# Half-size products of the second layer accumulated in PSUM, with copies on ScalarE and one wide addition; another order in the first layer's first step

## The chip, the cores and the metric

The kernel runs on one core of a Trainium2 chip. The metric is the device time of one execution in microseconds (us); less is better. An execution's time is a little more than the span from the first to the last instruction that the profile shows.

## The reference

```python
def _attn_ref(q, k, v, proj):             # 4 batches, 8 heads, 768 tokens, head size 64
    scale = 1.0 / np.sqrt(D)
    q_bits, k_bits = (einsum(x, proj) > 0 for x in (q, k))      # 6 bits each
    mask = q_bucket[:, :, :, None] == k_bucket[:, :, None, :]
    scores = np.where(mask, scale * q @ k.T, -1e9)
    attn = softmax(scores)
    return attn @ v

def _moe_ref(x, w_in, w_out):             # x: 3072 x 512, w_in: 512 x 2048, w_out: 2048 x 512
    h = x @ w_in
    g = h * (1.0 / (1.0 + np.exp(-1.702 * h)))
    return g @ w_out
```

The attention's output, transposed to (batch, token, head and feature), is the x of the feed-forward part. All of it is float32.

## The kernel before

**Three stages.** Attention fills the first 316 us. The first layer (`hidden`) runs to 606 us, in 24 steps: three blocks of 1024 tokens (`sb`) by eight blocks of 128 columns of each half of w_in (`mt`). The second layer (`product_of_halves`) takes the rest, in 21 steps: for each of the three token blocks the seven products `o` in the order `OUTER = (1, 2, 6, 7, 5, 3, 4)`. Numbered from 0, steps 0, 7 and 14 have o = 1, steps 5, 12 and 19 have o = 3, and steps 6, 13 and 20 have o = 4.

**Seven products instead of eight.** Both layers multiply matrices of 2 by 2 blocks with seven products, a scheme of the Strassen kind. Four sums of the left blocks and four of the right blocks are made first (`sums_a`, `sums_b`); the seven products are then combined by additions into the four output blocks c11, c12, c21, c22. The second layer does this twice, one scheme within the other: `OUTER` numbers the outer products, and each of them is made of seven inner products of half the size, `product(1)` to `product(7)`. `LEFT` and `RIGHT` say which block or sum each of these takes. Of the right operand, g: product 1 takes b11, 2 takes b21, 3 takes b22, 4 takes the sum t4, 5 takes t1, 6 takes t2, and 7 takes the second sum, which `sums_b` writes over b12. Of the left operand product 6 takes the sum s2 and product 3 the sum s4.

**One output step** (`product_of_halves(n, acc, after)`). Each inner product is eight TensorE instructions of 128 x 256 in the trace, into a bank of its own. ScalarE copies two of them out of PSUM (u and c12); VectorE combines the rest in half-size additions (128 x 256), and adds the quarters of an earlier product `acc` where the outer scheme wants that: o = 2, 6, 7, 3 and 4 have an acc, o = 1 and 5 have none. The result is `m`, four quarters of 128 x 256 in one of six buffers `wholes`.

**What stands between the products.** The callback `after(at)` places other VectorE work: `after(0)` runs what is pending from the step before (transposes of a finished block, `turned`, L831, and after o = 5 two wide additions, L991 and L992, the first of which is taken out ahead of the step with o = 3); `after(1)`, `after(2)` and `after(3)` make the sums of the next step's g, `g_sums(n + 1)`: t1 (L219), the second sum (L220), and then t2 (L221) and t4 (L222). In step 0 one sum goes to each of the four places. Finished blocks are written out by DMA (`written`, L838), and `fetch(n + 1)` (L806) loads the next g from DRAM into one of two buffers.

**Order of the work.** TensorE, VectorE, ScalarE and GpSimd (POOL) run their instructions in the order in which the program writes them (`tc.manual_schedule`); DMA issues on SyncE (SP) are ordered by the framework. GpSimd makes the sums of the left blocks (`inner_sums`, L211 to L214 for s1, s3, s2, s4). Before the GpSimd work of output steps 5 and 6 stands a one-element copy, so that this work waits for the product of the step before:

```python
                if n in (5, 6):
                    nc.gpsimd.tensor_copy(mark, ms[OUTER[n - 1]][0:1, 0, 0:1])
                for f in {0: inner_sums(4), 5: inner_sums(5) + inner_sums(6)[:2], 6: inner_sums(6)[2:]}.get(n, []):
```

Step 6 thus makes s2 and s4 of its own left operand.

**One hidden step.** `head(n)` makes product 1 and its copy u ahead of time, in the step before, so that product 6 can be accumulated onto the same bank; then 7 and 4 are accumulated there too, each after a copy by ScalarE (v, c22; c21 goes through the activation). Hidden step 0 has no step before it: its head stands directly ahead of product 6.

Of the kernel before, what the change touches and what calls it, by code (L numbers as in the profile page):

```python
# [38 lines left out]
def kernel(  # L39
# [17 lines left out]
    nc = tc.nc  # L57
# [8 lines left out]
    KC, FC = DM // P, FF // P  # L66
# [86 lines left out]
    for x in (0x3FFFFFFF, 0xFF800000):  # L153
        m = const.tile([P, 1], U32, name=f"mask_{x:x}")
# [61 lines left out]
    def sums_b(eng, b11, b12, b21, b22, t1, t2, t4):  # L216


        return [lambda: eng.tensor_tensor(t1, b12, b11, op=Alu.subtract),  # L219
                lambda: eng.tensor_tensor(b12, b22, b12, op=Alu.subtract),  # L220
                lambda: eng.tensor_tensor(t2, b22, t1, op=Alu.subtract),  # L221
                lambda: eng.tensor_tensor(t4, b21, t2, op=Alu.subtract)]  # L222
# [4 lines left out]
    def quarters_in(cols):  # L227
        w = [w_in_sb[:, K2 * k : K2 * (k + 1), F2 * i + cols.start : F2 * i + cols.stop]
             for i in range(2) for k in range(2)]
        return w + [s_in[:, i, :, cols] for i in range(3)]  # L230

    def quarters_x(sb):
        x = [xT[:, K2 * k : K2 * (k + 1), (2 * sb + j) * XT : (2 * sb + j + 1) * XT] for k in range(2) for j in range(2)]
        return x + [t_x[:, i] for i in range(3)]
# [460 lines left out]
    def feed_forward(tag, late=()):  # L695
# [3 lines left out]
        F4, TH = FC // 4, XT // 2  # L699
        n1 = N // (2 * XT)  # L700

        LEFT = dict(zip(range(1, 8), (0, 1, 6, 3, 4, 5, 2)))
        RIGHT = dict(zip(range(1, 8), (0, 2, 3, 6, 4, 5, 1)))
        OUTER = (1, 2, 6, 7, 5, 3, 4)
        with ExitStack() as fctx:
# [6 lines left out]
            def bank():  # L712
                turn[0] += 1
                return sets[turn[0] % 8 // 6 if len(sets) > 1 else 0].tile([P, XT], F32, tag="p", name="product")

            def product(ps, sb, mt, i, start=True):
                wq, xq = quarters_in(slice(mt * P, (mt + 1) * P)), quarters_x(sb)
                for kc in range(K2):
                    nc.tensor.matmul(ps, wq[LEFT[i]][:, kc, :], xq[RIGHT[i]][:, kc, :],  # L719
                                     start=(start and kc == 0), stop=(kc == K2 - 1), skip_group_check=not start)  # L720

            def head(n):

                ps, u = bank(), stage.tile([P, XT], F32, tag="u", name="u")
                product(ps, *divmod(n, FC // 2), 1)
                nc.scalar.copy(u, ps)  # L726
                return ps, u

            heads = {}

            def hidden(sb, mt, mid=(), end=()):
                n = sb * (FC // 2) + mt
                a, u = heads.pop(n) if n in heads else head(n)
                v, c12, c21, c22 = (stage.tile([P, XT], F32, tag=x, name=x) for x in ("v", "c12", "c21", "c22"))
                t2, t4 = (stage.tile([P, XT], F32, tag=x, name=x, bufs=1) for x in ("t2", "t4"))

                def keep(at, x):
                    loader[0].dma_start(out=g_dram[len(LEFT) * sb + at, :, mt, :], in_=x)

                def emit(c, at=None, of=None):  # L740
                    nc.scalar.activation(c, c if of is None else of, Act.Gelu_apprx_sigmoid)  # L741
                    if at is not None:
                        keep(at, c)

                product(a, sb, mt, 6, False)
                nc.scalar.copy(v, a)
                b = bank()
                product(b, sb, mt, 5)
                product(a, sb, mt, 7, False)
                nc.scalar.copy(c22, a)  # L750
                nc.vector.tensor_tensor(c22, b, c22, op=Alu.add)
                emit(c22, 3)
                c = bank()
                product(c, sb, mt, 2)
                nc.vector.tensor_tensor(u, c, u, op=Alu.add)
                emit(u, 0)
                if n + 1 < n1 * (FC // 2):
                    heads[n + 1] = head(n + 1)
                for x in mid:
                    x()  # L760
                product(a, sb, mt, 4, False)
                emit(c21, 2, a)
                product(b, sb, mt, 3, False)
                nc.vector.tensor_tensor(c12, b, v, op=Alu.add)  # L764
                emit(c12)

                for f, kept in zip(sums_b(nc.gpsimd, u, c12, c21, c22, v, t2, t4), ((4, v), (1, c12), (5, t2), (6, t4))):
                    f()
                    keep(*kept)
                for x in end:  # L770
                    x()
# [11 lines left out]
            def w_quarters(o):  # L783

                w = wqs[LEFT[o]]
                x = [w[:, i, F4 * j : F4 * (j + 1), :] for i in range(2) for j in range(2)]
                at = OUTER.index(o)
                if at == 0:
                    return x[0:2] + rooms[3:4] + x[3:] + rooms[0:3]
                return x + rooms[3 * at + 1 : 3 * at + 4]  # L790
# [8 lines left out]
            steps_out = [(sb, o) for sb in range(n1) for o in OUTER]  # L799
# [40 lines left out]
            def product_of_halves(n, acc, after):  # L840

                sb, o = steps_out[n]
                wq, gq = w_quarters(o), g_quarters(n)
                m = wholes[n % len(wholes)]
                u, v = (gp.tile([P, TH], F32, tag=x, name=x, bufs=2) for x in ("u", "v"))
                c11, c12, c21, c22 = (m[:, i] for i in range(4))

                def product(i):
                    ps = bank()[:, 0:TH]
                    for c in range(F4):  # L850
                        nc.tensor.matmul(ps, wq[LEFT[i]][:, c, :], gq[RIGHT[i]][:, c, :], start=(c == 0), stop=(c == F4 - 1))  # L851
                    return ps

                def add(dst, x, y):
                    nc.vector.tensor_tensor(dst, x, y, op=Alu.add)  # L855

                def corner():
                    add(c11, product(2), u)
                    if acc is not None:
                        add(c11, c11, acc[:, 0])  # L860


                final = n + 1 == len(steps_out)
                nc.scalar.copy(u, product(1))  # L864
                if not final:
                    corner()
                nc.scalar.copy(c12, product(3))
                after(0)
                add(v, product(6), u)
                add(c21, product(7), v)  # L870
                if acc is not None:
                    add(v, v, acc[:, 1])
                    add(c22, c21, acc[:, 3])
                    add(c21, c21, acc[:, 2])
                add(c12, c12, v)
                after(1)
                p = product(5)
                add(c22, p, c21 if acc is None else c22)
                add(c12, p, c12)
                after(2)  # L880
                if final:
                    corner()
                    after(4)
                add(c21, product(4), c21)
                after(3)
                return m
# [14 lines left out]
            for sb in range(n1):  # L901
                for mt in range(MT):
                    n = sb * MT + mt
# [45 lines left out]
            for n, (sb, o) in enumerate(steps_out):  # L949
                final = n + 1 == len(steps_out)  # L950
# [8 lines left out]
                m = wholes[n % len(wholes)]  # L959

                def after(at):
                    if at == 0:
                        while pending:
                            pending.pop(0)()

                    steps = [later_sums[at : at + 1]] if n == 0 else [[], later_sums[0:1], later_sums[1:2], later_sums[2:], []][at : at + 1]

                    if n + 2 >= len(steps_out):
                        turns = [lambda q=q: turned(m, int(final), int(not final), q, q + 1) for q in range(4)]
                        if final:  # L970
                            steps = [[[], [], [turns[1], turns[3]], [turns[2]], [turns[0]]][at]]
                        elif at == 3:
                            steps = [later_sums[2:3], turns[0:2], turns[3:4], later_sums[3:], turns[2:3]]
                    for f in sum(steps, []):
                        f()
                    if final and at in (2, 3):
                        written(sb, 0, (3 - at,), loader + [nc.scalar])
                    if n + 2 == len(steps_out) and at == 3:
                        written(sb, 1, (0, 1), loader + [nc.scalar])

                acc = {6: 1, 7: 6, 2: 1, 3: 6, 4: 7}.get(o)
# [70 lines left out]
```

## Time and profile before

| | |
|---|---|
| median of 3 runs | 873.26 us (872.33 to 873.48) |
| the profiled execution | 872.87 us |
| its span | 871.0 us |
| granted TensorE clock, mean | 0.997 |
| TensorE busy, its matmuls of the first layer (L719), of the second (L851) | 857.9 us, 33% and 26% of the chain |
| VectorE, ScalarE, GpSimd busy | 661.4, 340.2, 311.6 us |
| output steps 1, 2, 6, 8 | 12.08, 14.04, 12.45, 12.08 us |

The span is the time from the first to the last instruction; what an execution takes beyond it lies outside the program's instructions. A busy TensorE is not TensorE at its peak. In output steps 1 to 20 the step's time is counted from the first matmul of its product 1 to that of the next step's.

### The profile page before, as it was taken

To read this page: it belongs to the slowest core of one execution; us is meant where nothing else is said; L and a number is where in the kernel's file an instruction comes from. 1 tells how busy PE (TensorE), PEld (TensorE's weight loads), DVE (VectorE), ACT (ScalarE), POOL (GpSimd) and SP (SyncE) were. 2 spreads that over 40 slices of the span, in tenths; PEclk is the share of its full clock that TensorE was granted. 3 is DMA by queue.
4 is the path that set the end of the run, shared out by engine and by line. 5 is a ranking of instruction groups with operands and counts; after the bars stand their busy time and mean duration, and the time that the engine had idled before them with its cause. 6 is when DMAs were issued, how large, how long until landed. Compare 5 with 4: busy or idle time off the path is not lost.

```text
span 871.0 us, 13350 instructions
## 1 busy us (share of the span) xinstructions
PE 857.9 (99%) x4845; PEld 499.2 (57%) x4845; DVE 661.4 (76%) x924; ACT 340.2 (39%) x567; POOL 311.6 (36%) x275
## 2 busy tenths in 40 slices
PE   9999999999999999999999999999999999999996
PEld 5444444444444444444444444445878888888885
DVE  4589999999999875457555556676788977897786
ACT  5866667776666643434334333433000000000000
POOL 4242234333223465665443344559903100000000
PEclk9999999999999999999999999999999999999998
DMA  5636645456652104665456655576744675467524
GB/s 127 96 57 109 104 84 85 84 99 117 99 97 61 56 2 157 205 208 181 172 198 197 217 181 172 190 254 223 271 156 158 199 243 201 163 209 243 194 97 99
DMA packets 169161, 132.09 MB, mean 152 GB/s; under 512 B 123616, under 2 KB 138112, under 8 KB 163712
## 3 DMA queue, kind: packets, MB, share of 16 engines
q1 hardware_dynamic: 166528, 129.70, 52.5%
q10 hardware_dynamic: 2560, 1.46, 0.8%
q8 instruction: 40, 0.66, 0.3%
q14 instruction: 33, 0.27, 0.1%
HBM read 79.69 MB, written 50.33 MB: 149 GB/s over the span
## 4 chain that ended last, share of the span: by engine, by line
PE 95%; DVE 3%; issue 0%; DMA 0%; ACT 0%; ACTq 0%; DVEq 0%
PE product L719 33%; PE product L851 26%; PE ps L432 18%; PE av L465 15%; DVE xT L855 1%; PE dn L486 1%; PE hash L408 1%; PE tp L366 1%; DVE y L831 1%; DMA k<-in_k_dram 0%; DVE v L855 0%; PE hash L373 0%; DVE t2a L221 0%; DVE raw_g L220 0%; ACTq L838 0%
## 5 line engine op out<-in xcount | busy, mean ns | idle before, releaser
L433 ACT ACTIVATE e<-ps 128x768 f32<-128x768 f32 x192 | 151.2, 812 | 25.7 <-PE ps L432 23.2
L432 PE MATMUL ps<-qT,kT 64*128 64x384 f32 x768 | 155.1, 482 | 0.0
L465 PE MATMUL av<-e,v 128*32 128x385 f32 x1536 | 128.0, 487 | 0.0
L719 PE MATMUL product<-xT,w_in_sb 128*128 128x512 f32 x288 | 127.8, 592 | 0.0
L440 POOL TENSOR_TENSOR acc<-e 128x768 f32<-128x768 f32 x32 | 51.7, 1617 | 194.4 <-ACT e L433 175.0
L719 PEld LDWEIGHTS product<-xT,w_in_sb 128*128 128x128 f32 x288 | 54.6, 190 | 69.0 <-issue 68.5
L465 PEld LDWEIGHTS av<-e,v 128*32 128x32 f32 x1536 | 48.6, 109 | 76.2 <-issue 74.9
L432 PEld LDWEIGHTS ps<-qT,kT 64*128 64x128 f32 x768 | 68.0, 187 | 38.5 <-issue 38.4
L719 PE MATMUL product<-t_x,s_in 128*128 128x512 f32 x192 | 86.4, 592 | 0.8 <-ACT u L726 0.8
L764 DVE TENSOR_TENSOR c<-product,v 128x512 f32<-128x512 f32 x24 | 16.6, 690 | 90.8 <-PE product L719 90.8
L219 POOL TENSOR_TENSOR v<-c,u 128x512 f32<-128x512 f32 x24 | 32.3, 1345 | 128.1 <-ACT c L741 128.1
L864 ACT COPY u<-product 128x256 f32<-128x256 f32 x21 | 7.8, 372 | 174.1 <-PE product L851 140.9
L719 PEld LDWEIGHTS product<-t_x,s_in 128*128 128x128 f32 x192 | 36.4, 190 | 47.1 <-issue 45.2
L432 PE MATMUL ps<-qf,kf 64*128 64x384 bf16 x384 | 62.9, 324 | 0.1
L741 ACT ACTIVATE c<-c 128x512 f32<-128x512 f32 x48 | 30.3, 630 | 72.3 <-DVE c L764 43.7
L441 POOL TENSOR_TENSOR acc<-acc,e 128x768 f32<-128x768 f32 x32 | 55.8, 1745 | 2.5
L446 DVE SCALAR_TENSOR_TENSOR acc<-e 128x768 f32<-128x768 f32 x32 | 47.7, 1489 | 5.1 <-ACT e L433 5.1
L719 PE MATMUL product<-t_x,w_in_sb 128*128 128x512 f32 x96 | 45.1, 592 | 0.0
L719 PE MATMUL product<-xT,s_in 128*128 128x512 f32 x96 | 45.1, 592 | 0.0
L750 ACT COPY c<-product 128x512 f32<-128x512 f32 x24 | 14.1, 586 | 66.3 <-PE product L719 66.3
L432 PEld LDWEIGHTS <-kf 64*128 64x128 bf16 x384 | 18.9, 94 | 35.1 <-issue 6.2
L448 DVE TENSOR_TENSOR acc<-acc,e 128x768 f32<-128x768 f32 x32 | 34.3, 1071 | 3.3
(206 smaller groups left out, 1513.4 us busy)
## 6 DMA issues: line engine op xcount, KB each, us to landing
raw_g<-g_dram SPq DMA_DIRECT2D x22, 1024.0 KB
s_in<-g_dram SPq DMA_DIRECT2D x20, 1024.0 KB
g_dram<-c SPq DMA_DIRECT2D x72, 256.0 KB
g_dram<-t SPq DMA_DIRECT2D x48, 256.0 KB
raw<-in_moe_w_in_dram SPq DMA_DIRECT2D x16, 512.0 KB
raw<-in_moe_w_out_dram SPq DMA_DIRECT2D x16, 512.0 KB
v<-in_v_dram SPq DMA_DIRECT2D x32, 192.0 KB
g_dram<-u SPq DMA_DIRECT2D x24, 256.0 KB
```

The costliest lines, as they stand in the source:

```text
L219: return [lambda: eng.tensor_tensor(t1, b12, b11, op=Alu.subtract), lambda: eng.tensor_tensor(b12, b22, b12, op=Alu.subtract), lambda: eng ...
L432: nc.tensor.matmul(ps[:, j, 0:HS], a[hs, keys], m[hs, cols], start=not last, stop=last)
L433: nc.scalar.activation(es[c][:, kt, :, 0:HS], ps[:, :, 0:HS], Act.Exp, scale=1.0 / D**0.5)
L440: nc.gpsimd.tensor_tensor(acc, es[c][:, 0, :, 0:HS], es[c][:, 1, :, 0:HS], op=Alu.add)
L441: nc.gpsimd.tensor_tensor(acc, acc, es[c][:, 2, :, 0:HS], op=Alu.add)
L446: nc.vector.scalar_tensor_tensor(acc, e[0], T * TINY, e[1], op0=Alu.add, op1=Alu.add)
L448: nc.vector.tensor_tensor(acc, acc, x, op=Alu.add)
L465: nc.tensor.matmul(av[D * j + d : D * j + d + 32, :], vt[:, t, j, d : d + 32], es[c][:, t, j, :], start=(t == 0), stop=(t == T - 1))
L719: nc.tensor.matmul(ps, wq[LEFT[i]][:, kc, :], xq[RIGHT[i]][:, kc, :], start=(start and kc == 0), stop=(kc == K2 - 1), skip_group_check=not ...
L741: nc.scalar.activation(c, c if of is None else of, Act.Gelu_apprx_sigmoid)
L764: nc.vector.tensor_tensor(c12, b, v, op=Alu.add)
L851: nc.tensor.matmul(ps, wq[LEFT[i]][:, c, :], gq[RIGHT[i]][:, c, :], start=(c == 0), stop=(c == F4 - 1))
```

## The change

In an output step (all but the last) products 1, 6, 7 and 4 are accumulated in one bank, one onto the other. ScalarE copies the bank's content out after each of them: u, v, c22, c21. Products 2, 3 and 5 have banks of their own and are added to the copies by VectorE. The order of the products becomes 1, 2, 6, 3, 7, 5, 4 (before: 1, 2, 3, 6, 7, 5, 4). Where there is an acc, its four quarters are added to `m` in one VectorE instruction of 128 x 1024 behind product 4, instead of in four of 128 x 256 in the course of the step. The places of `after(0)` to `after(3)` follow the products as shown. The last step keeps its order: 1, 3, 6, 7, 5, 2, 4.

In hidden step 0 product 5 is made ahead of product 6, and the head of step 1 stands between products 6 and 7 instead of behind product 2.

```diff
+                b = bank()
+                if n == 0:
+                    product(b, sb, mt, 5)
                 product(a, sb, mt, 6, False)
                 nc.scalar.copy(v, a)
-                b = bank()
-                product(b, sb, mt, 5)
+                if n == 0:
+                    heads[1] = head(1)
+                else:
+                    product(b, sb, mt, 5)
                 product(a, sb, mt, 7, False)
                 nc.scalar.copy(c22, a)
                 nc.vector.tensor_tensor(c22, b, c22, op=Alu.add)
...
-                if n + 1 < n1 * (FC // 2):
+                if n and n + 1 < n1 * (FC // 2):
                     heads[n + 1] = head(n + 1)
...
-                def product(i):
-                    ps = bank()[:, 0:TH]
+                def product(i, onto=None):
+                    ps = bank()[:, 0:TH] if onto is None else onto
                     for c in range(F4):
-                        nc.tensor.matmul(ps, wq[LEFT[i]][:, c, :], gq[RIGHT[i]][:, c, :], start=(c == 0), stop=(c == F4 - 1))
+                        nc.tensor.matmul(ps, wq[LEFT[i]][:, c, :], gq[RIGHT[i]][:, c, :], start=(onto is None and c == 0),
+                                         stop=(c == F4 - 1), skip_group_check=onto is not None)
                     return ps
...
+                if n + 1 < len(steps_out):
+                    a = product(1)
+                    nc.scalar.copy(u, a)
                     add(c11, product(2), u)
+                    product(6, a)
+                    nc.scalar.copy(v, a)
+                    add(c12, product(3), v)
+                    after(0)
+                    product(7, a)
+                    nc.scalar.copy(c22, a)
+                    after(1)
+                    p = product(5)
+                    add(c22, p, c22)
+                    add(c12, p, c12)
+                    after(2)
+                    product(4, a)
+                    nc.scalar.copy(c21, a)
                     if acc is not None:
-                        add(c11, c11, acc[:, 0])
+                        add(m, m, acc)
+                    after(3)
+                    return m
...
```

What is left of the old body is the last step's; it loses only the branches that it never takes.

More of the change, by code (lines that the diff above doesn't have):

```diff
@@ L855, in add @@
                     nc.vector.tensor_tensor(dst, x, y, op=Alu.add)
-                def corner():
+                if n + 1 < len(steps_out):
+                    a = product(1)
+                    nc.scalar.copy(u, a)
                     add(c11, product(2), u)
+                    product(6, a)
[11 more added lines that the diff above has]
+                    nc.scalar.copy(c21, a)
                     if acc is not None:
-                        add(c11, c11, acc[:, 0])
-                final = n + 1 == len(steps_out)
+                        add(m, m, acc)
+                    after(3)
+                    return m
                 nc.scalar.copy(u, product(1))
-                if not final:
-                    corner()
                 nc.scalar.copy(c12, product(3))
@@ L870, in product_of_halves @@
                 add(c21, product(7), v)
[L871 to L874, printed above, removed]
+                add(v, v, acc[:, 1])
+                add(c22, c21, acc[:, 3])
+                add(c21, c21, acc[:, 2])
                 add(c12, c12, v)
@@ L877, in product_of_halves @@
                 p = product(5)
-                add(c22, p, c21 if acc is None else c22)
+                add(c22, p, c22)
                 add(c12, p, c12)
                 after(2)
-                if final:
-                    corner()
-                    after(4)
+                add(c11, product(2), u)
+                add(c11, c11, acc[:, 0])
+                after(4)
                 add(c21, product(4), c21)
```

## The prediction

> **What bounds the kernel now.** I read the page first: engine shares, then the chain of work that ended last.
>
> ```profile
> PE 857.9 (99%) x4845; PEld 499.2 (57%) x4845; DVE 661.4 (76%) x924; ACT 340.2 (39%) x567; POOL 311.6 (36%) x275
> ...
> PE 95%; DVE 3%; issue 0%; DMA 0%; ACT 0%; ACTq 0%; DVEq 0%
> ```
>
> TensorE is the bound; the change leaves its matmuls as they are. So only TensorE's pauses and the tail can move the time. The waits of PE give two that touch the changed lines:
>
> ```profile
> PE product L851 <- DVE t2a L221: 1.7, 1, 1.7
> PE product L719 <- ACT u L726: 0.8, 1, 0.8
> ```
>
> Next, busy time by stretch, one stretch for an output step (first column after the stretch is its length):
>
> ```profile
> 618.23:630.31 12.08, 12.08 (x57) 10.64 (x56) 9.95 (x13) 0.74 (x2) 11.85 (x8) 1.00 0.85 308
> 630.31:644.35 14.04, 12.33 (x58) 10.56 (x57) 13.80 (x22) 0.74 (x2) 2.15 (x2) 1.00 0.51 186
> ...
> 680.61:693.06 12.45, 12.32 (x58) 10.56 (x56) 12.18 (x23) 0.74 (x2) 0.00 (x0) 1.00 0.46 150
> ```
>
> A step without a pause is 12.08 us, seven products of 1.725. Counting from 0, step 2 is 1.95 longer, step 6 0.37. Last, the timeline where steps meet, in light step 8 and around step 5:
>
> ```profile
> 705.50 0.41 DVE L855 TENSOR_TENSOR xT<-product,xT 128x256 f32<-128x256 f32 x1
> 705.84 1.21 DVE L221 TENSOR_TENSOR t2a<-raw_g,t1a 128x1024 f32<-128x1024 f32 x1
> ...
> 710.33 1.89 PE L851 MATMUL product<-t2a,w_in_sb 128*128 128x256 f32 x8
> ...
> 675.84 1.22 DVE L992 TENSOR_TENSOR t_x<-t_x,xT 128x1024 f32<-128x1024 f32 x1
> 675.98 1.11 POOL L955 COPY mark<-t_x 1x1 f32<-1x1 f32 x1 [5.80 <-DVE t_x L855]
> 677.05 1.27 POOL L213 TENSOR_TENSOR s_in<-w_in_sb,w_out_sb 128x512 f32<-128x512 f32 x1
> ```
>
> Read the first three with S = 705.15, the step's start: product 6, the fourth, starts at S+5.18 and reads t2, which VectorE ended at S+1.90. That slack is what the new order spends. The last three show POOL's little mark copy stretched to 1.11 beside a wide VectorE addition (its other one took 0.17), and then the sum s2 that stands behind it.
>
> **What goes and comes.** VectorE loses, in a step with an earlier product to add (acc), eleven half additions of some 0.42 and gets four plus one wide one (L991, same shape: 1.22): 4.6 becomes 2.9. ScalarE goes from two copies of 0.37 to four, in a stage where it is busy 0.74 of 12.08. None of that is on TensorE's path, so it earns nothing by itself. The copies stand between products on one bank: copy v ends some 0.6 after product 6 and product 7 comes 1.73 after it, since product 3 lies between; without that cover each would cost TensorE about 0.6. Accumulating at full rate is seen already: L719's product 4 onto a used bank is at 328.04, the next at 329.76, 1.72 for four matmuls, like the rest.
>
> **Hidden step 0.** Product 1 starts at 316.59; product 6 waits for copy u until 319.38 (1.08 more than 1.715 per product), and product 7 comes 0.08 late. With product 5 ahead, copy u (over at 319.23) is done before product 6 at 320.0, and the moved head covers copy v. Product 5's inputs were there (POOL's s1 ended at 313.75). The moved head issues four matmuls and one copy, no DMA, and is queued ahead of nothing that TensorE lacked. **-1.15**; all later stages follow TensorE.
>
> **Light steps.** In the new order product 6 is third, at S'+3.45, its weight load 0.22 earlier at S'+3.23 (S' is the start of the next step). Ahead of t2 VectorE now has the wide addition, which waits for product 4 and ScalarE's copy: copy starts S'+0.20 (a copy at 710.53 behind a product whose successor started at 710.33), ends +0.57, wide addition +0.60, t2 one pitch of 1.13 later (850.75 to 851.88 in the chain), ends +2.95; the load follows 0.12 later (637.22 to 637.34 in step 2), +3.07. **0**, with 0.16 to spare, and the step 2 pause shows 0.11 more (load 2.06 late, product 7 late by 1.95). Queued behind the waiting addition are t2 and t4 alone; t4 is needed last.
>
> **Step 2** (ends the 1.95 pause). In step 1 VectorE's half additions and POOL's sums stretch each other (1.48 for one of 0.42). New: product 5 ends, c22 at 628.79, c12 629.13, the second sum (it overwrites b12) 629.47. That takes 2.2 beside POOL (t1 took 2.28 at 666.77), the wide addition partly so, 1.6; t2 ends at 634.4, load 634.5 against 633.54: 0.96 late, 0.86 after the 0.11. **-1.1**; free of POOL t2 ends at 632.9 (-1.95), fully beside it 635.4 (-0.1). I take the middle since POOL's sums ended at 632.54.
>
> **Heavy steps 5, 12, 19** (o = 3): the pending wide addition and four transposes now come after product 3, which is fourth. From S: c12 at 7.10, +0.34, addition to transposes 1.26 (843.10 to 844.36), transposes 1.86, t1 1.13, c22 and c12 0.34 each, second sum 1.13, wide 1.13, t2 1.21: it ends at S+15.84 = S'+3.76, load S'+3.88, 0.65 late, less 0.11: **+0.55** at step 13 (bounds 0.3 and 0.9). At step 20 VectorE is the chain to the end, and there t2 starts at S'+2.55 = 852.74 where the chain has
>
> ```profile
> 850.75 1.13 DVE raw_g L220
> ...
> 852.21 1.13 DVE t2a L221
> ```
>
> (timeline: 852.13): **+0.6** on everything behind it (0.3 to 1.0).
>
> **Step 6.** POOL's mark (L955) reads c11 of the product before. That was final early in step 5; now the wide addition writes it last, at S'+2.63 = 683.24. Behind the mark stand s2 and s4 of this very step, and product 6 needs s2. Mark 1.11 as in the row, beside t2: 684.4; s2 beside t4 2.13 (a POOL sum beside VectorE at 668.05): 686.5; load 686.65 instead of 683.84, 2.7 after the 0.11, against 0.37 before: **+2.3**. With mark at 0.17 and s2 at 1.27 it is +0.5; s4 arrives in time for product 3 either way. [...]
>
> **Sum.** -1.15 - 1.1 + 0.55 + 0.6 + 2.3 = +1.2. The profiled execution took 872.87 (span 871.0, 1.87 around it), so 874.1; the median of the runs, 873.26, is 0.39 above it: 874.5.
>
> **Rivals.**
> - *Slower: step 2's pause stays.* If the second sum and the wide addition both run fully beside POOL, that term is -0.1 and the sum +2.2: 875.5. For it: 8 POOL instructions fill 11.85 of step 1's 12.08. Against: VectorE's work there shrinks. 0.2.
> - *Slower: t2 late in the light steps too.* Eleven of them have the wide addition ahead; it decides once t2 ends beyond S'+3.22. Were it 0.2 beyond that, 2.2 in all: 876.7. Against: 0.27 of slack from rows. [...] 0.12.
> - *Slower: transfers.* The y writes leave some 3.5 us later (787.9 for 784.41); if the fetch of raw_g is queued behind, t1 of step 15 waits and t2 comes up to 1.2 late: 875.7. Against: the fetch is ready first, at the end of product 7. 0.08.
> - *Faster.* POOL lets the mark and s2 through (+0.5), step 2's pause goes wholly (-1.95), heavy terms at their lower ends (0.6): -2.0, 871.3. 0.12.
> - *The new first step doesn't remove its wait* (product 5 or 6 lacks an input): +1.15, 875.6. All its inputs were there by 316.3. 0.03.
>
> **How the numbers follow.** About 0.2%, 1.75 us, is what a measurement can tell from no change. The forecast, +1.2, lies within; it has 0.45. Sums between the cases spread over the edges: faster 0.13, same 0.46, slower 0.41. All low ends add to -2.0, all high ends (0.8 for 1.15 in hidden step 0, 1.2 for transfers) to +4.9; both at once are unlikely, so the range is 871.4 to 877.6. The likeliest case's own is 872.6 to 875.0.
>
> **What would show it.** Hidden step 0 without the ACT u wait; step 2 some 13 us; step 6 some 14.8, with PE waiting for POOL L213; steps 13 and 20 waiting for t2 about half a microsecond; light steps at 12.08. I am wrong if PE waits for t2 in most steps, if step 6 is under 13.3 long, or if VectorE's lighter load shortens anything but step 2.

## The result and the profile after

The changed kernel took 878.80 us in the median of four runs (877.59 to 880.01), the kernel before 872.92 (872.33 to 873.48): ratio 1.0067, 95% interval 1.005 to 1.0085. It is slower by 5.9 us, where 1.2 was forecast, and lies beyond the range given. The profiled execution took 878.14, its span is 876.2, 5.2 more than before. So the ledger below is made against 5.2.

The page of the changed kernel, busy time of the engines, and then the waits of PE (total in us, times, longest):

```profile
PE 860.7 (98%) x4845; PEld 499.7 (57%) x4845; DVE 632.3 (72%) x822; ACT 355.2 (41%) x607; POOL 313.7 (36%) x275
```

```profile
PE product L856 <- DVE t2a L221: 2.4, 2, 2.1
PE product L856 <- POOL s_in L213: 1.5, 1, 1.5
...
PE product L856 <- DVE t2b L221: 0.4, 1, 0.4
...
PE product L856 <- DMA raw_g<-g_dram: 0.2, 1, 0.2
```

(The chain on this page is followed back over the last part of the span alone, so its shares are not compared with those of before.) VectorE has 29 us less to do and ScalarE 15 more, as meant. TensorE has as many matmuls as before, and yet 2.8 us more of busy time. The wait for ACT u L726 is gone, the wait for t2 has stayed, and a wait for POOL's s2 (L213) is new. Busy time by stretch, one stretch for output steps 1, 2, 6 and 8 (length, then PE, PEld, DVE, ACT, POOL, PEclk, DMA share, GB/s):

```profile
617.02:629.49 12.47, 12.25 (x58) 10.45 (x56) 4.33 (x5) 1.67 (x5) 12.09 (x9) 1.00 0.78 276
629.49:645.72 16.23, 14.12 (x57) 11.84 (x58) 12.14 (x17) 1.31 (x4) 2.32 (x1) 0.89 0.44 158
682.04:696.42 14.38, 12.62 (x58) 10.48 (x56) 11.32 (x16) 1.49 (x4) 4.46 (x3) 1.00 0.41 145
708.51:720.59 12.08, 12.08 (x57) 10.64 (x56) 5.52 (x8) 1.49 (x4) 0.00 (x0) 1.00 0.98 291
```

In step 2 PE is busy 14.12 for work that takes 12.09, and the granted clock (PEclk) is 0.89: that is where most of the additional busy time comes from. Where each microsecond lies, as time over plain steps, steps without a pause, of 12.09 (the two rows ahead of step 1 and the row of step 20 with the tail give whole lengths):

| | before | after | change | forecast |
|---|---|---|---|---|
| attention (first matmul of the first layer) | 316.59 | 316.43 | -0.16 | 0 |
| first layer to the start of the second | 289.55 | 288.50 | -1.05 | -1.15 |
| step 1 | 0 | +0.38 | +0.38 | 0 |
| step 2 | +1.95 | +4.14 | +2.19 | -1.1 |
| step 5 | 0 | +0.07 | +0.07 | 0 |
| step 6 | +0.36 | +2.29 | +1.93 | +2.3 |
| step 9 | 0 | +0.37 | +0.37 | 0 |
| step 13 | 0 | +0.61 | +0.61 | +0.55 |
| step 20 and the tail | 20.78 | 21.63 | +0.85 | +0.6 |
| sum | | | +5.2 | +1.2 |

Steps 1 and 2 came to +2.57 where -1.1 was forecast. That is 3.7 of the 4.0 us by which the sum was off. All other terms are within 0.4 of theirs.

### The profile page after: what moved, and what is told of

Its sections match the earlier page's. It is cut to its first block, busy times and chain, and to the rows that moved or that the text cites. A ratio compares the mean times of both kernels' runs of the same rounds, so it can differ in the third digit from the quotient of the medians.

```text
span 876.2 us, 13348 instructions
## 1 busy us (share of the span) xinstructions
PE 860.7 (98%) x4845; PEld 499.7 (57%) x4845; DVE 632.3 (72%) x822; ACT 355.2 (41%) x607; POOL 313.7 (36%) x275
## 5 line engine op out<-in xcount | busy, mean ns | idle before, releaser
L448 DVE TENSOR_TENSOR acc<-acc,acc 128x768 f32<-128x768 f32 x32 | 31.2, 974 | 6.3 <-POOL acc L441 3.2
```

The source lines that it names most:

```text
L448: nc.vector.tensor_tensor(acc, acc, x, op=Alu.add)
```

## The experiments

The theory after the two traces: the accumulation itself costs nothing, and the loss is made of pauses around t2 and s2 and of a slower clock behind the longest pause. Its rival: the accumulated products and the copies between them cost TensorE time.

### The two halves of the change by themselves

The kernel before with the new order of hidden step 0:

```diff
+                b = bank()
+                if n == 0:
+                    product(b, sb, mt, 5)
                 product(a, sb, mt, 6, False)
...
```

> The kernel before with the new order of hidden step 0 alone. Theory (the ledger of the two traces): TensorE's 1.15 us in hidden step 0 go and nothing later moves, so 1.2 us less than before, some 871.7. Rival (what is gained there is waited for again in the second layer, because the GpSimd sums and the g transfers at the seam do not come earlier): the pause of output step 2 grows from 1.95 and the time is that of before, within 0.3.

871.53 us (11 runs), ratio 0.9984, interval 0.9974 to 0.9993: 1.4 less. The first layer takes 288.50 instead of 289.55, and step 2 has its 1.94, step 6 its 0.36, as before. What is gained at the first step is kept. Its timeline:

```profile
315.75 1.98 PE L719 MATMUL product<-xT,w_in_sb 128*128 128x512 f32 x4
317.57 3.60 PE L719 MATMUL product<-t_x,s_in 128*128 128x512 f32 x8
317.81 0.59 ACT L726 COPY u<-product 128x512 f32<-128x512 f32 x1 [0.44 <-PE product L719]
```

Eight matmuls (products 5 and 6) follow product 1 without a pause, and the copy u lies beside product 5.

The other half, the changed second layer with the old hidden step 0 (against the changed kernel):

```diff
                 b = bank()
-                if n == 0:
-                    product(b, sb, mt, 5)
+                product(b, sb, mt, 5)
...
-                if n and n + 1 < n1 * (FC // 2):
+                if n + 1 < n1 * (FC // 2):
```

> The changed kernel with hidden step 0 in its old order. Theory: the second layer alone carries the whole loss, 5.2 + 1.2 = 6.4 us over before in the span, some 879.3, with step 2 again the largest part. Rival (the earlier arrival of the second layer is what makes the transfer of step 2's g late): step 2's pause is under 1.5, no slow clock, and the time is 875 to 876.

878.86 us, ratio 1.0074 (1.0058 to 1.0089). Its profiled span is 5.5 over before, not 6.4: step 1 has +1.53, a wait of TensorE for the transfer of g, step 2 +2.04, with a pause of 1.86 and no slow matmul (granted clock 0.997 in the mean, as before), and step 6, with +2.30, is the largest part instead of step 2. So the second layer carries the loss, and how steps 1 and 2 share it differs from run to run.

### Step 6: who reads what the wide addition writes

```diff
-                    nc.gpsimd.tensor_copy(mark, ms[OUTER[n - 1]][0:1, 0, 0:1])
+                    nc.gpsimd.tensor_copy(mark, ms[5][0:1, 0, 0:1])
```

> The changed kernel; the one-element copy ahead of step 6's GpSimd sums reads the product of step 4 instead of that of step 5, so it no longer waits for the wide addition. Theory: step 6 falls from 14.38 to about 12.6 (t2 alone is then 0.6 late), 1.8 us less in all. Rival (s2 and s4 are late for another reason, or accumulating costs TensorE the time): step 6 stays at 14.4.

Step 6 falls from 2.29 to 1.39 over a plain step (to 13.48, where about 12.6 was expected), and TensorE no longer waits for POOL there. It waits for t2 instead (its t1 was late too, at 681.06 and 1.97 long beside POOL's sums that now run there). The median is 877.83, only 1.0 under the changed kernel, in runs that scatter by 2 (877.01 to 879.06); the profile is of the slowest of them. In the changed kernel (timeline):

```profile
683.50 1.25 DVE L861 TENSOR_TENSOR t_x<-t_x,xT 128x1024 f32<-128x1024 f32 x1
...
684.82 1.11 POOL L973 COPY mark<-t_x 1x1 f32<-1x1 f32 x1 [12.71 <-DVE t_x L861]
685.89 1.25 POOL L213 TENSOR_TENSOR s_in<-w_in_sb,w_out_sb 128x512 f32<-128x512 f32 x1
...
687.20 1.99 PE L856 MATMUL product<-t2a,s_in 128*128 128x256 f32 x8 [1.54 <-POOL s_in L213]
687.22 2.13 POOL L214 TENSOR_TENSOR s_in<-w_out_sb,s_in 128x512 f32<-128x512 f32 x1
...
689.41 1.99 PE L856 MATMUL product<-raw_g,s_in 128*128 128x256 f32 x8 [0.22 <-POOLq L1033]
```

The wide addition ends at 684.75, the mark starts 0.07 later and takes 1.11 beside t2 (0.17 with the early mark), s2 follows, and product 6 starts when s2 is there. Up to there that is the chain that was forecast. The last two lines were not: s4 takes 2.13 and ends at 689.35, and product 3, which reads it, starts 0.06 later, behind a second pause.

### t2 ahead of the wide addition

```diff
-                    steps = [later_sums[at : at + 1]] if n == 0 else [[], later_sums[0:1], later_sums[1:2], later_sums[2:], []][at : at + 1]
+                    steps = [later_sums[at : at + 1]] if n == 0 else [[], later_sums[0:1], later_sums[1:3], later_sums[3:], []][at : at + 1]
...
-                            steps = [later_sums[2:3], turns[0:2], turns[3:4], later_sums[3:], turns[2:3]]
+                            steps = [turns[0:2], turns[3:4], later_sums[3:], turns[2:3]]
```

> The changed kernel with the sum t2 ahead of the wide addition instead of behind it. Theory: t2 is ready 1.13 earlier in every step: steps 9 and 13 at 12.1, the pause of step 2 about 1.2 instead of 2.4 and without the slow clock, so step 2 at 13.3 instead of 16.2; step 6 some 1.1 longer, since the copy on GpSimd waits for the wide addition that now comes later; the tail as it is. In all 2.5 to 3 us less. Rival (the accumulation's copies pace TensorE): steps 2, 9 and 13 stay as they are.

Steps 9 and 13 have no excess left, and the pause of step 2 is 1.04 with no slow matmul: step 2 at +1.22 instead of +4.14. Step 6 grew by 2.3, not 1.1, to +4.62: its pause became 2.83 long, and seven slow matmuls followed it (the profiled execution's granted clock is 0.993 in the mean). Step 1 has +1.23, a wait for the transfer, and step 20 with the tail is 0.96 longer than in the changed kernel; neither was expected. The median is 877.20, 1.6 less than the changed kernel, not 2.5 to 3.

### The quarters of the wide addition

```diff
                     add(c11, product(2), u)
+                    if acc is not None:
+                        add(c11, c11, acc[:, 0])
...
-                        add(m, m, acc)
+                        add(c21, c21, acc[:, 2])
```

(the same behind c12 and c22)

> The changed kernel with the wide addition split into its four quarters, each directly behind the quarter that it completes; only c21's stays behind product 4. Theory: t2 is ready 0.8 earlier, c11 is final early in the step, so the copy on GpSimd in step 6 waits no longer: step 6 near 12.5, step 13 at 12.1, the tail 0.6 shorter, step 2's pause under 2 and without the slow clock; 4 to 5 us less than the changed kernel, 874. Rival (accumulating in one bank costs the time): no more than 1 us less.

875.06 us, 3.7 less than the changed kernel, ratio to before 1.0026 (1.0017 to 1.0036). The slow clock is gone: behind step 2's pause of 1.48 eight matmuls span 1.97 and the next eight 1.89. But steps 6 and 13 have +1.68 and +0.58: the quarter additions in front of t2 in the heavy steps cost about what t2 gained, and step 6 now waits for t2 instead of s2. The expectations that step 13 would be plain, step 6 near 12.5 (it is 13.77) and the tail 0.6 shorter (it is as long as in the changed kernel) failed.

### Step 2: transfer, VectorE or clock

Without the fetch of g for step 2 (that step works on old data):

```diff
-                if 0 < n and n + 1 < len(steps_out):
+                if 1 < n and n + 1 < len(steps_out):
                     fetch(n + 1)
```

> The changed kernel without the fetch of g for output step 2 (that step works on old data). Theory (in step 1 the sum t1, and with it all that leads to t2, waits for this transfer): t1 of step 1 starts 0.4 after product 3, near 624.5 instead of 629.5, no wait for a transfer at the start of step 2, steps 1 and 2 together 0.9 to 1.5 over two plain steps instead of 4.5, no slow clock; 3 us less in all. Rival (VectorE beside the GpSimd sums is what is late, as the prediction had it): the pause before product 6 stays at 2 us or more.

The transfer's wait is gone, t1 starts at 624.06, as expected; the pause isn't, it is 2.27 long, and seven slow matmuls follow (eight span 2.92, the next eight 2.66, and the granted clock of the step is 0.89). Steps 1 and 2 have +4.03. The median is 877.48, 1.3 less than the changed kernel, not 3. The theory that the transfer alone makes VectorE late fell, and the timeline shows what takes its place:

```profile
629.72 2.28 DVE L861 TENSOR_TENSOR xT<-xT 128x1024 f32<-128x1024 f32 x1
...
631.00 2.12 POOL L214 TENSOR_TENSOR w_in_sb<-xT,w_in_sb 128x512 f32<-128x512 f32 x1
631.93 2.28 DVE L221 TENSOR_TENSOR t2a<-raw_g,t1a 128x1024 f32<-128x1024 f32 x1
...
634.35 2.92 PE L856 MATMUL product<-t2a,w_in_sb 128*128 128x256 f32 x8 [2.11 <-DVE t2a L221]
```

While VectorE waits for the transfer, POOL's sums run at 1.27 each but for the last, which takes 2.32 and is over at 631.82, and the wide addition and t2 then take 1.21. Without the wait they run beside POOL and take 2.28 each. Either way t2 ends late, 5.7 us into step 2 with the wait and 5.6 without it.

Product 2 of step 2 made once more, into an unused bank, ahead of the late product 6:

```diff
                     add(c11, product(2), u)
+                    if n == 2:
+                        product(2)
                     product(6, a)
```

> The changed kernel with product 2 of step 2 made a second time, into an unused bank, ahead of the late product 6: 1.73 us of work for TensorE in the pause. Theory (the slow matmuls come from the pause itself): the last product before t2 ends 1.7 later, the pause is some 0.6, no matmul takes 0.43, and step 2 is 1.7 shorter than in the changed kernel's profile. Rival (the clock drops for a reason of its own): slow matmuls are there still, step 2 as long as it was.

Of the pause 1.02 is left, and no matmul takes 0.43; PEclk is 1.00 over the whole step (15.01 long with the 1.73 of filler, so 1.2 shorter than step 2 of the changed kernel although the filler is in it). The median is 877.11, 1.7 less than the changed kernel: by the medians the kernel that does this work twice is the faster one, though the intervals of the two against before (1.0031 to 1.006, and 1.005 to 1.0085) overlap. What the run shows clearly is in its trace, the full clock behind the shorter pause.

The kernel before with t1 for step 2 made twice in step 1:

```diff
                     for f in sum(steps, []):
                         f()
+                    if n == 1 and at == 1:
+                        later_sums[0]()
```

> The kernel before with the sum t1 for step 2 made twice in step 1, so that VectorE is 1.1 us later there and the pause before product 6 of step 2 grows from 1.87 to about 3.0. Nothing else is touched. Theory (a pause over some 2 us drops TensorE to half speed for a while): about eight matmuls of 0.43 instead of 0.216 behind the pause, step 2 at 16.8 instead of 14.0, the time 2.8 over before. Rival (no clock effect): step 2 at 15.2, the time 1.1 over before.

875.81, 3.2 over before, ratio 1.0035 (1.002 to 1.0049). The pause grew to 2.44, not 3.0, and step 2 to +4.24; step 1 has +0.56, most of it a wait for the transfer. Its busy time by stretch:

```profile
635.00:638.00 3.00, 0.93 (x5) 0.48 (x3) 3.00 (x5) 0.37 (x1) 0.00 (x0) 1.00 0.00 0
638.00:639.00 1.00, 0.79 (x2) 0.73 (x3) 0.96 (x2) 0.00 (x0) 0.00 (x0) 0.54 0.00 0
639.00:640.00 1.00, 1.00 (x3) 0.78 (x3) 0.97 (x3) 0.00 (x0) 0.00 (x0) 0.50 0.00 0
640.00:641.00 1.00, 1.00 (x4) 0.77 (x3) 1.00 (x4) 0.00 (x0) 0.00 (x0) 0.50 0.65 115
641.00:642.00 1.00, 1.00 (x5) 0.86 (x4) 1.00 (x4) 0.00 (x0) 0.00 (x0) 0.75 0.93 303
```

The last column but two is the granted clock: half speed for some 3.4 us behind the pause, in a kernel whose second layer accumulates nothing. So the clock follows the pause, not the change.

### Versions that repair it

Mark and t2 repaired together (the two edits above):

> The changed kernel with both: t2 ahead of the wide addition, and the copy ahead of step 6's GpSimd sums reading the product of step 4. Theory: step 6 at 12.1 to 12.3, steps 9 and 13 at 12.1, steps 1 and 2 some 2.4 over two plain steps, no slow clock; the median 872.5 to 874, level with the kernel before. Rival (the accumulation itself costs TensorE time in every step): 876 or more.

874.55, ratio 1.0022 (1.0012 to 1.0031), a little over what was expected. Step 6 is at +0.25, steps 9 and 13 are plain, no slow matmul; steps 1 and 2 have +1.08 and +1.38, the first a wait for the transfer. Steps 3 to 19 thus run plain but for 0.25 with all products accumulated as in the change. The rival, TensorE time lost in every step, falls. Step 20 with the tail is not plain: it has 22.67 against 20.78 before.

The same with the fetch for step 2 issued from ScalarE's queue:

```diff
-                    fetch(n + 1)
+                    fetch(n + 1, nc.scalar if n == 1 else None)
```

> As the one with both repairs, and the fetch of g for step 2 is issued from ScalarE's queue, where it doesn't stand behind the writes of the last hidden sums (on SyncE it is issued at 620.0, ScalarE is free for it at 617.6). Theory: no wait of TensorE for that transfer at the start of step 2, step 1 at 12.1, step 2 about 13.2 as VectorE then runs beside the GpSimd sums: 1 us less than without. Rival (the transfer is late for its bandwidth, which it shares with the next fetch): no difference.

871.45, ratio 0.9989 (0.998 to 0.9998): 3.1 less, not 1. It is issued at 617.25 instead of 620, step 1 is plain, and step 2 has +0.15 (12.23 long, not 13.2): with t1 done early, all that stands between product 5 and t2 is the second sum. A step 20 with tail of 22.6 (before: 20.8) is what is left against the best kernels. Its matmuls are plain; from the start of the last one to the end of the span it takes 10.7 against 8.9. VectorE's last transpose ends 0.8 later there, and the end of the span, behind the last writes, comes another 1.0 later still. Why, no run here resolves.

The kernel before with the new hidden step 0 and t2 one place earlier (again the edits above):

> The kernel before with the new order of hidden step 0, and t2 one place earlier, ahead of product 4 and c21's half addition. Theory: t2 comes 0.34 earlier in each step: step 2's pause 1.6 instead of 1.95, step 6 without its 0.36; 870.8, 0.7 less than with the first step alone. Rival (the second sum's end, not the place of t2, sets it): 871.5.

870.92, ratio 0.998 (0.9971 to 0.9989). Step 6 is plain and step 2 has +1.63, as expected; against the first step alone, 871.53 in another set of runs, 0.6 less (0.35 when each is taken against the runs of before in its own set).

Last, the hybrid: the kernel before, the new hidden step 0, t2 one place earlier, output step 1 alone in the changed form, and the early fetch:

```diff
+                if n == 1:
+                    a = product(1)
+                    nc.scalar.copy(u, a)
+                    add(c11, product(2), u)
+                    product(6, a)
...
```

> The kernel before with the new order of hidden step 0, t2 ahead of product 4, output step 1 alone in the changed form (accumulated products, one wide addition behind t2), the others as before with product 6 fourth, and the fetch for step 2 from ScalarE's queue. Theory: VectorE has 1.7 us less to do in step 1, where it runs beside the GpSimd sums, and t2 stands ahead of the wide addition, so it is ready some 4.4 us into step 2 at the latest, before product 6 needs it at 5.0: no pause in step 2, no 0.36 in step 6; 2.3 less than with the first step alone, some 869.3. Rival (beside the GpSimd sums VectorE is late in any form): a pause of 1 us or more is left.

869.34, ratio 0.9958 (0.9944 to 0.9972): 3.4 under before and 9.5 under the changed kernel. Steps 1 and 2 in its stretches:

```profile
617.68:629.77 12.09, 12.09 (x57) 10.64 (x56) 9.34 (x12) 1.12 (x3) 11.86 (x7) 1.00 0.87 293
629.77:641.86 12.09, 12.09 (x58) 10.64 (x56) 11.88 (x17) 1.12 (x3) 4.48 (x3) 1.00 0.51 184
```

No step of the second layer has a pause any more, and the tail is 20.76.

## Why the prediction was wrong

**What bounds the kernel** was right but for one thing: TensorE's pauses and the tail moved the time, and the lighter VectorE earned nothing by itself (step 8 has 5.52 us of VectorE work and is 12.08 long, as before). But the matmuls behind step 2's pause were slower too (0.43 instead of 0.216), and for that there was no term.

**Hidden step 0**, -1.15: measured -1.05, and shown alone at -1.4 in the median.

**Light steps**, 0: right but for step 9, whose 0.37 came from a transfer (below). Step 3 of the changed kernel, which starts at 645.72 behind a step with the wide addition (timeline):

```profile
646.32 1.23 DVE L861 TENSOR_TENSOR xT<-xT 128x1024 f32<-128x1024 f32 x1 [0.17 <-ACT xT L879]
647.46 1.22 DVE L221 TENSOR_TENSOR t2b<-s_in,t1b 128x1024 f32<-128x1024 f32 x1
...
649.17 1.89 PE L856 MATMUL product<-t2b,w_in_sb 128*128 128x256 f32 x8
```

The wide addition starts 0.60 into the step and t2 ends 2.96 into it, where 0.60 and 2.95 were forecast; product 6 starts at 3.45, not late. The slower rival about the light steps fell. In steps 2 and 6 the larger instruction did come late, and splitting it brought 3.7 us in all, some 1.7 of them (an estimate from the seven slow matmuls) because the slow clock went with the pause.

**Step 2**, -1.1: this is the step that failed, by two terms. First, t2 was to end 4.1 into the step and ended 5.7 into it (635.17 against a start at 629.49). I took the middle between a VectorE free of POOL and one beside it; measured was 0.6 past even the far end (635.4, which is 5.1 into the step). In the changed kernel the wait for g did it, 4.84 us ahead of t1; where that wait is taken away it is POOL, 2.28 for an instruction of 1.21, and t2 is hardly earlier. The new place of t1, and so a wait for g at that place, was not looked at: before, t1 began 2.4 us into step 2 and found its data there, while now VectorE was free for it at 624.63, 4.9 us ahead of step 2. The same transfer made step 1's 0.38. Second, the price of a pause was taken to be its length. The pause of 2.28 was followed by seven matmuls of 0.43 instead of 0.216 and one in between: 1.7 more, so that step 2 had 4.14. The timeline of the kernel before, then timeline and clock of the changed kernel:

```profile
632.75 1.21 DVE L219 TENSOR_TENSOR t1a<-raw_g 128x1024 f32<-128x1024 f32 x1
```

```profile
629.47 1.22 DVE L219 TENSOR_TENSOR t1a<-raw_g 128x1024 f32<-128x1024 f32 x1 [4.84 <-DMA raw_g<-g_dram]
...
633.96 1.21 DVE L221 TENSOR_TENSOR t2a<-raw_g,t1a 128x1024 f32<-128x1024 f32 x1
...
635.32 2.88 PE L856 MATMUL product<-t2a,w_in_sb 128*128 128x256 f32 x8 [2.11 <-DVE t2a L221]
...
638.00 2.70 PE L856 MATMUL product<-raw_g,w_in_sb 128*128 128x256 f32 x8
```

```profile
636.00:637.00 1.00, 1.00 (x4) 0.83 (x4) 0.84 (x2) 0.00 (x0) 0.00 (x0) 0.61 0.00 0
637.00:638.00 1.00, 1.00 (x4) 0.73 (x3) 0.00 (x0) 0.00 (x0) 0.00 (x0) 0.50 0.00 0
```

Eight matmuls of 128 x 256 span 2.88 and 2.70 where they span 1.89 at full clock (step 3 above). No case of the prediction had a clock in it. 1.6 (t2), 0.4 (step 1) and 1.7 (clock) make the 3.7 by which steps 1 and 2 were off. Without the 1.7 the profiled execution would have taken some 876.4 (an estimate, 878.14 less 1.7), inside the range: the term that was left at nothing took it out. Of the signs that the prediction named, "step 2 some 13 us" is the one that clearly didn't come; it is 16.23.

**Step 6**, +2.3: measured +1.93, and the nearness is in part luck, since two errors offset each other. The mark was 1.11 long as forecast, and s2 stood behind it. But s2 took 1.25 beside VectorE's t4, not 2.13, and t4 took 2.23: s2 began at 685.89, t4 at 685.99, and here the one that began first kept its length. Of the 2.29 in step 6, some 1.8 is the delay of product 6, and less the 0.37 of before that leaves some 1.45 where 2.3 was forecast. The other 0.5 is s4, which started beside t4, took the 2.13 and held up product 3; the prediction had it "in time for product 3 either way". The sum of the high ends, +4.9, uses 2.7 for this step: no run shows that term, and the changed kernel showed +1.93 in its place.

**Heavy steps**, +0.55 at step 13 and +0.6 at the end: measured +0.61 and +0.85. In the tail:

```profile
857.12 1.25 DVE L221 TENSOR_TENSOR t2a<-raw_g,t1a 128x1024 f32<-128x1024 f32 x1
```

t2 starts 2.59 into step 20, forecast 2.55.

**Transfers**: the rival held, in a smaller form and in another place. In step 8 t1 waited 2.05 for the g that stood behind the y writes, and the second sum 0.65, so that t2 came 0.37 late for step 9. It was priced at up to 1.2 around step 15. The wait for g in step 1, above, is of the same kind and cost more.

## What to carry to other kernels

The wide operation at the step's end was cheap here by its busy time (VectorE has 29 us less to do) and dear by its place (3.7 us, by the run that splits it): ask which small readers of its output (here a one-element copy) and which late instructions of the next step (here t2) now stand behind it, and move those ahead of it. When an operation is moved forward, look at everything that it reads, the transfers too, at its new time. Don't price every pause of the matmul engine by its length alone: here those up to 1.9 us cost their length, and those from 2.3 us cost some 1.7 more in the profiled executions, though, by an estimate, not in every execution (below).

## What the hardware showed that was not expected

TensorE's clock fell to half for some 3.4 us behind a pause in five of five profiles that had a pause of 2.27 to 2.83 us between matmuls: changed kernel (pause 2.28, clock 0.50 from 636.22 to 639.63), longer pause (2.44, the stretches above), without the fetch (2.27, clock of the step 0.89), and, read from slow matmuls or the mean clock, t2 ahead (2.83, mean 0.993) and early mark (2.81, mean 0.995, of which by an estimate the half speed behind the last matmul takes 0.003 and the fall 0.002). Where the longest pause in the second layer was 1.87 or less no fall is shown: the trace of the kernel before has none ahead of its last matmul, step 2 is at 1.00 with the filler, and the mean clocks of these profiles are 0.996 to 0.998.

The length of the pause may not be the whole of it. In the trace of the changed kernel the first clock record begins at 8.16, and the clock changes at 636.22 (to 0.50), at 639.63 (back) and, behind the last matmul, at 871.74 (to 0.50): 184, 1 and 68 times 3.413 us apart. In that of the kernel before, the first record begins at 8.49 and the one fall, behind the last matmul, is at 865.24, 251 times 3.413 us later. Cut into stretches of that length, TensorE's records leave 2.11 us idle in the stretch that ends with the fall at 636.22, and 3.41 and 2.80 in those that end with the falls behind the last matmul; behind the stretches with 1.54 or less neither trace has a fall. The pause of the changed kernel lay inside one stretch (2.11 idle); the 1.87 of the kernel before was cut into 0.89 and 0.82. From these two traces comes an estimate that no run tests: the same pause can cost 1.7 us more in one execution and not in the next, as such stretches happen to lie. The runs with t2 ahead of the wide addition suggest just that: those of 878.69 (the profiled one, with the fall) and 878.15 us have a mean clock of 0.993 and 0.995, those of 876.20 and 876.26 have 0.997. The half speed after the last matmul takes 0.0025 off the mean in the changed kernel and 0.0033 in the kernel before, and the fall inside the second layer 0.002 more, so that, by an estimate from these, the last two had none. How often the changed kernel itself meets the fall isn't known.
